# adaLN attention block: K from centred x only, 1/sigma on the scores, scale in three parts, shift by column tiles, P turned by DMA

## The chip, the core and the metric

The kernel runs on one core of a Trainium2 chip. Its engines are TensorE (PE, with its weight loads PEld), VectorE (DVE), ScalarE (ACT), GpSimd (POOL) and SyncE (SP), which issues nearly all DMAs. The engines run side by side and meet through semaphores. The metric is the device time of one execution in microseconds (us), the median of the runs.

## The reference

```python
B, N, D = (2, 256, 1152)
def reference(x, c, wqkv, wo, w_mod):
    mod = (_silu(c) @ w_mod).reshape(B, 6, 1, D)
    shift_a, scale_a, gate_a, ... = [mod[:, i] for i in range(6)]
    h = _layernorm(x, axis=-1) * (1 + scale_a) + shift_a
    qkv = h @ wqkv                                   # D x 3D
    q, k, v = (qkv[..., :D], qkv[..., D:2 * D], qkv[..., 2 * D:])
    p = _softmax(jnp.einsum('bqd,bkd->bqk', q, k) * D ** (-0.5), axis=-1)
    a = jnp.einsum('bqk,bkd->bqd', p, v) @ wo
    return x + gate_a * a
```

All tensors are bf16. The layer norm is x minus its mean, divided by sigma (with eps 1e-5). One head spans all 1152 columns. Of the six thirds of `w_mod` only shift, scale and gate of the attention are used.

## The kernel before

The 512 tokens (two batches of 256) lie in four tiles `t` of 128; batch 0 is tiles 0 and 1. The 1152 columns are nine blocks `k` of 128. PE contracts over `k`, so h is needed transposed: `hT[:, k, tokens]`.

Each engine carries out its instructions in the order in which the code states them. The wrappers `vec`, `sca`, `ten` and `spq` record every instruction of DVE, ACT, PE and SP, and `pin` (at the end) ties each list into that order. All of them therefore have the line of the wrapper, L74, in the profile; they are told apart by their tiles. POOL's instructions have their own lines. PSUM has eight banks: a pool `psum` of six and two single ones, `psum_a` and `psum_b`; a new tile waits until the tile that had its bank before has been read.

The stages, in PE's order:

- *Start.* c is loaded as 18 rows of 128, turned on PE, and made into silu(c) (`silu_c`). Twelve filler products keep PE busy meanwhile. For each tile of x, mean and variance come from DVE (`dve_stats`, `dve_aggr`) or, for tile 3, from ACT (`act_mean`, `act_var`); POOL computes 1/sigma with a power of -0.5 (L197, L198, L223 to L226); `dve_norm` writes the normalised x, PE turns it (`transposes`), and DVE or ACT copies it to `xnT`.
- *Scale.* 1 + scale is a product of w_mod's second sixth (`wS`) with silu(c), for the first four column blocks (`scale_A`) and the other five (`scale_B`), 81 products of 54 columns (silu(c) repeated 27 times).
- *K.* `scaled` writes `hTs`, the normalised x times (1 + scale), without shift: a shift adds the same amount to all scores of a query, which the softmax removes. Six of K's nine column blocks are summed in six banks at a time (`k_part`, `k_step`); two more are begun early (`early_half`, added from SBUF afterwards), and the last is a whole `k_block`.
- *Shift.* 81 products of 54 columns (`shift_block`) with `wH`, w_mod's first sixth, stand among K's last products. Then `modulated` writes `hT` from `xnT`, scale and shift, 12 of 18 half blocks on DVE and 6 on ACT.
- *Q*, nine blocks of nine products; the *scores* S, 36 products of 256 columns; *V*, twelve groups (`v_group`) of nine products of 384 columns.
- *Softmax* on DVE and ACT beside V: `row_max`, `exps`, `normalized`. P is turned by eight PE transposes ahead of the last V group, and copied to SBUF.
- *Gate.* DVE multiplies w_mod's third sixth (`wG`) with silu(c) block by block: 18 steps `gate_step` on 128 x 1152, which add into `gacc`. Twelve stand ahead of the first row maximum, two between the softmax steps, four behind. After the last one POOL sums over the partitions (two `PARTITION_ALL_REDUCE`, L558), which gives `gate_bc`, and then writes `wo_last` (L579), the last 192 columns of wo times the gate of batch 1, in nine instructions.
- *P times V*, 36 products, gives `attnT`; the *output*, per tile three chunks of 384 columns; DVE multiplies with the gate (`ga`) and adds x (`o_sb`). The last tile's last 192 columns use `wo_last`, so that they need only x; the last 64 get x by PE and are copied by ACT.

SP issues the loads in the order x, wS, wK, wH, then Q's first columns, wG, the rest of Q and V, and wo. wG takes the place of wS and wO that of wH, so these loads wait until PE has used the older weights. The stores follow on the same queue.

Of the kernel before, what the change touches and what calls it, by code (L numbers as in the profile page):

```python
# [16 lines left out]
def kernel(  # L17
# [10 lines left out]
    P = 128  # L28
# [6 lines left out]
    NCH = D // CW  # L35
    EPS = 1e-5
# [3 lines left out]
    NEARLY = 2  # L40
    WE = (NACC + NEARLY) * P
    KA = 4
    KB = KT - KA
    NR = 54
# [4 lines left out]
    wmod_v = w_mod.rearrange("(kk p) (s n) -> p kk s n", p=P, s=6)  # L49
# [6 lines left out]
    work = ctx.enter_context(tc.tile_pool(name="work", bufs=2))  # L56
    psum = ctx.enter_context(tc.tile_pool(name="psum", bufs=6, space=PSUM))
# [5 lines left out]
    pe_seq, dve_seq, act_seq, sp_seq = [], [], [], []  # L63
# [20 lines left out]
    spq = _Rec(nc.sync, sp_seq)  # L84

# [11 lines left out]

    ident = const.tile([P, P], BF16)
    nc.gpsimd.memset(ident, 0.0)
    nc.gpsimd.affine_select(  # L100
# [3 lines left out]
    junk_rhs = const.tile([P, 512], BF16)  # L104
    vec.memset(junk_rhs, 1.0)
    ones_bf = const.tile([P, P], BF16)
    nc.gpsimd.memset(ones_bf, 1.0)
    ones_row = const.tile([1, 512], BF16)
    nc.gpsimd.memset(ones_row, 1.0)
    neg_half = const.tile([P, 1], F32)  # L110
    nc.gpsimd.memset(neg_half, -0.5)

    c_sb = const.tile([2 * KT, P], BF16)
    x_sb = act.tile([P, TT, D], BF16)
    nc.scalar.preload_act_table_set("natural_log_exp_and_others")
    nc.scalar.dma_start(out=c_sb, in_=c.rearrange("b (k p) -> (b k) p", p=P))
# [4 lines left out]
    wmpool = ctx.enter_context(tc.tile_pool(name="wmpool", bufs=1))  # L123
# [8 lines left out]

    def load_k(k0, k1, c0=0, c1=D):
        spq.dma_start(out=wK[:, k0:k1, c0:c1], in_=wqkv_v[:, k0:k1, D + c0 : D + c1])

    PAIRS = ((0, 2), (2, 4), (4, 6), (6, 8), (8, 9))
    CA = KA * P
    load_x(1)
    load_x(0)
    load_x(3)  # L140
    for k0, k1 in PAIRS:
        load_mod(wS, 1, k0, k1, 0, CA)
    load_k(0, 1, 0, WE)
    load_x(2)
    for k in range(1, KA):
        load_k(k, k + 1, 0, WE)
    load_mod(wS, 1, 0, 5, CA, D)
    load_mod(wS, 1, 5, KT, CA, D)
    load_k(KA, 6)
    load_k(6, KT)  # L150
    load_k(0, KA, WE, D)
    for k0, k1 in PAIRS:
        load_mod(wH, 0, k0, k1, 0, D)


    cT_ps = psum_b.tile([P, 2 * KT], BF16, tag="pb")
    ten.transpose(cT_ps, c_sb, ident[: 2 * KT, : 2 * KT])
    junk_ps = psum_a.tile([P, 512], F32, tag="pa")

    def fillers(n):  # L160
        for _ in range(n):
            ten.matmul(junk_ps, lhsT=ident, rhs=junk_rhs, start=True, stop=True)

    fillers(12)
    e_sb = small.tile([P, 2 * KT], F32, tag="e_sb")
    sca.activation(out=e_sb, in_=cT_ps, func=ACT.Exp, scale=-1.0)
    scT_f = const.tile([P, KT, B], F32)
    scT_rep = const.tile([P, KT, NR // B, B], BF16)

    def silu_c():  # L170
        vec.tensor_scalar_add(out=e_sb, in0=e_sb, scalar1=1.0)
        vec.reciprocal(out=e_sb, in_=e_sb)
        vec.tensor_tensor(
            out=scT_f.rearrange("p k b -> p b k"),
            in0=cT_ps.rearrange("p (b k) -> p b k", b=B),
            in1=e_sb.rearrange("p (b k) -> p b k", b=B),
            op=ALU.mult,
        )
        sca.copy(out=scT_rep, in_=scT_f.unsqueeze(2).to_broadcast([P, KT, NR // B, B]))
# [3 lines left out]


    mv_all = const.tile([P, TT, 2], F32)
    rstd = const.tile([P, TT], F32)
    nb = const.tile([P, TT], F32)
    xn = act.tile([P, TT, D], BF16, tag="a1")
    xnT = act.tile([P, KT, T], BF16, tag="a2")
    stats = {t: small.tile([P, NCH, 6], F32, tag="stats", name="stats") for t in (1, 0, 2)}  # L190

    def dve_stats(t, s):
        vec.bn_stats(out=stats[t][:, s, :], in_=x_sb[:, t, s * CW : (s + 1) * CW])

    def dve_aggr(t):
        vec.bn_aggr(out=mv_all[:, t, :], in_=stats[t])
        nc.gpsimd.tensor_scalar_add(out=rstd[:, t : t + 1], in0=mv_all[:, t, 1:2], scalar1=EPS)  # L197
        nc.gpsimd.tensor_tensor(out=rstd[:, t : t + 1], in0=rstd[:, t : t + 1], in1=neg_half, op=ALU.pow)  # L198

    def dve_nb(t):  # L200
        vec.scalar_tensor_tensor(
            out=nb[:, t : t + 1], in0=mv_all[:, t, 0:1], scalar=-1.0, in1=rstd[:, t : t + 1],
            op0=ALU.mult, op1=ALU.mult,
        )

    def dve_norm(t):
        vec.tensor_scalar(
            out=xn[:, t, :], in0=x_sb[:, t, :], scalar1=rstd[:, t : t + 1], scalar2=nb[:, t : t + 1],
            op0=ALU.mult, op1=ALU.add,
        )  # L210

    ssum = small.tile([P, 1], F32, tag="ssum")
    nmean = small.tile([P, 1], F32, tag="nmean")
    ssq = small.tile([P, 1], F32, tag="ssq")

    def act_mean(t):
        sca.activation(out=xn[:, t, :], in_=x_sb[:, t, :], func=ACT.Copy, accum_out=ssum)
        sca.activation(out=nmean, in_=ssum, func=ACT.Copy, scale=-1.0 / D)

    def act_var(t):  # L220
        sca.activation(out=xn[:, t, :], in_=x_sb[:, t, :], func=ACT.Square, bias=nmean,
                       scale=1.0, accum_out=ssq)
        nc.gpsimd.tensor_scalar(out=rstd[:, t : t + 1], in0=ssq, scalar1=1.0 / D, scalar2=EPS,  # L223
                                op0=ALU.mult, op1=ALU.add)
        nc.gpsimd.tensor_tensor(out=rstd[:, t : t + 1], in0=rstd[:, t : t + 1], in1=neg_half, op=ALU.pow)
        nc.gpsimd.tensor_tensor(out=nb[:, t : t + 1], in0=nmean, in1=rstd[:, t : t + 1], op=ALU.mult)  # L226

    tps = {}
    HALF = ((0, KA), (KA, KT))

    def transposes(t, h, pool, tag):
        k0, k1 = HALF[h]
        tp = pool.tile([P, KB, P], BF16, tag=tag, name="tp")
        for k in range(k0, k1):
            ten.transpose(tp[:, k - k0, :], xn[:, t, k * P : (k + 1) * P], ident)
        tps[t, h] = tp

    def xnT_copy(t, h, on_dve):
        k0, k1 = HALF[h]
        dst, srct = xnT[:, k0:k1, t * P : (t + 1) * P], tps[t, h][:, : k1 - k0, :]  # L240
        if on_dve:
            vec.tensor_copy(out=dst, in_=srct)
        else:
            sca.copy(out=dst, in_=srct)


    s1p = const.tile([P, KT, B], F32)
    sh = const.tile([P, KT, B], F32)
# [3 lines left out]
    early = const.tile([P, NEARLY, T], F32)  # L252

    junk_mm = psum.tile([P, 512], F32, tag="mm")

    def fillers2(n):
        for _ in range(n):
            ten.matmul(junk_mm, lhsT=ident, rhs=junk_rhs, start=True, stop=True)

    psSA = psum_a.tile([P, KA - 1, NR], F32, tag="pa")  # L260
    ten.matmul(psSA.rearrange("p j r -> p (j r)"), lhsT=ones_bf[0:1, :],
               rhs=ones_row[0:1, 0 : (KA - 1) * NR], start=True, stop=False, skip_group_check=True)
    psS0 = psum_b.tile([P, NR], F32, tag="pb")
    ten.matmul(psS0, lhsT=ones_bf[0:1, :], rhs=ones_row[0:1, 0:NR], start=True, stop=False,
               skip_group_check=True)

    def scale_A(kk):
        for j in range(KA):
            ten.matmul(
                psS0 if j == 0 else psSA[:, j - 1, :], lhsT=wS[:, kk, j * P : (j + 1) * P], rhs=sc_rhs(kk),  # L270
                start=False, stop=(kk == KT - 1), skip_group_check=True,
            )

    def scale_B(kk):
        for j in range(KA, KT):
            ten.matmul(
                psSB[:, j - KA, :], lhsT=wS[:, kk, j * P : (j + 1) * P], rhs=sc_rhs(kk),
                start=(kk == 0 and j == KA), stop=(kk == KT - 1), skip_group_check=True,
            )

    def shift_block(kk):
        for j in range(KT):
            ten.matmul(
                psH[:, j, :], lhsT=wH[:, kk, j * P : (j + 1) * P], rhs=sc_rhs(kk),
                start=(kk == 0 and j == 0), stop=(kk == KT - 1), skip_group_check=True,
            )

    def one(t):
        return slice(t * P, (t + 1) * P)

    def scaled(k, sl, scalar):
        vec.tensor_scalar(out=hTs[:, k, sl], in0=xnT[:, k, sl], scalar1=scalar, scalar2=None, op0=ALU.mult)

    def k_part(k, sl, first=False):
        for f in range(NACC):
            ten.matmul(
                accs[f][:, sl], lhsT=wK[:, k, f * P : (f + 1) * P], rhs=hTs[:, k, sl],
                start=first, stop=False, skip_group_check=True,
            )
# [22 lines left out]
    def evac(idx, out_ap, in_ap):  # L322
        if idx % 2 == 0:
            return vec.tensor_copy(out=out_ap, in_=in_ap)
        return sca.copy(out=out_ap, in_=in_ap)
# [337 lines left out]
```

## Time and profile before

| | |
|---|---|
| median of 3 runs | 100.06 us (100.00 to 100.22) |
| profiled execution, first to last instruction | 99.5 us |
| PE / DVE / ACT / POOL busy | 92.7 / 66.8 / 29.3 / 24.5 us |
| DMA | 21.06 MB, in the slices up to 400 GB/s until 55 us |
| 81 Q products of 512 columns | 17.65 us from 35.16 |
| 16 gate steps `SCALAR_TENSOR_TENSOR` | 1.42 us each |
| two `PARTITION_ALL_REDUCE` | 6.89 us each |

The profiled execution is given by its span alone. A row of the timeline has the start, the time from the first to the last of the merged instructions, engine, line, operation, output <- inputs with their shapes, the number of instructions, and in brackets the engine's idle time before them and what ended it. Matmuls overlap: a 512-column product is shown with some 0.38 us, but the next one starts 0.216 us later, so spacings count and not means. In the 40 slices each digit is the busy share in tenths of 2.49 us.

### The profile page before, as it was taken

To read this page: it belongs to the slowest core of one execution; us is meant where nothing else is said; L and a number is where in the kernel's file an instruction comes from. 1 tells how busy PE (TensorE), PEld (TensorE's weight loads), DVE (VectorE), ACT (ScalarE), POOL (GpSimd) and SP (SyncE) were. 2 spreads that over 40 slices of the span, in tenths; PEclk is the share of its full clock that TensorE was granted. 3 is DMA by queue.
4 is the path that set the end of the run, shared out by engine and by line. 5 is a ranking of instruction groups with operands and counts; after the bars stand their busy time and mean duration, and the time that the engine had idled before them with its cause. 6 is when DMAs were issued, how large, how long until landed. Compare 5 with 4: busy or idle time off the path is not lost.

```text
span 99.5 us, 1843 instructions
## 1 busy us (share of the span) xinstructions
PE 92.7 (93%) x753; PEld 57.3 (58%) x753; DVE 66.8 (67%) x131; ACT 29.3 (29%) x58; POOL 24.5 (25%) x29
## 2 busy tenths in 40 slices
PE   0899999899999999999999999999999999999960
PEld 0334788894465644444447866566568766556560
DVE  1694398426063899999992999960237767879870
ACT  5340905402060494223322453323126400000000
POOL 5042043000000000000000000039999910079600
PEclk9999999999999999999999999999999999999999
DMA  2999999999999999999999300000000000302212
GB/s 59 319 259 368 403 395 407 386 394 414 382 370 389 359 403 377 342 326 327 347 410 412 127 0 0 0 0 0 0 0 10 0 0 0 119 5 114 88 70 85
DMA packets 16339, 21.06 MB, mean 212 GB/s; under 512 B 1355, under 2 KB 10827, under 8 KB 16331
## 3 DMA queue, kind: packets, MB, share of 16 engines
q1 hardware_dynamic: 16160, 20.93, 59.7%
q8 instruction: 6, 0.10, 0.4%
q10 hardware_dynamic: 171, 0.02, 0.1%
q14 instruction: 2, 0.02, 0.0%
HBM read 19.76 MB, written 1.18 MB: 210 GB/s over the span
## 4 chain that ended last, share of the span: by engine, by line
PE 86%; DVE 6%; DMA 2%; POOL 1%; issue 1%; ACT 0%; DVEq 0%
PE ps L74 59%; PE acc L74 12%; PE s_ps L74 4%; DVE stats L74 3%; PE tp L74 2%; PE psH L74 2%; DMA c_sb<-in_c_dram 2%; PE psE L74 2%; PE junk_mm L74 2%; PE psSB L74 1%; PE psSA L74 1%; DVE o_sb L74 1%; DVE ga L74 1%; POOL rstd L198 1%; DVE mv_all L74 0%
## 5 line engine op out<-in xcount | busy, mean ns | idle before, releaser
L558 POOL PARTITION_ALL_REDUCE gate_bc<-gacc x2 | 13.7, 6886 | 49.8 <-DVE gacc L74 49.8
L74 DVE SCALAR_TENSOR_TENSOR gacc<-wG,scT_f,gacc 128x1152 f32<-128x1152 bf16 x16 | 22.7, 1418 | 0.5
L74 PE MATMUL ps<-wqv,hT 128*128 128x384 bf16 x108 | 17.9, 326 | 0.0
L74 PE MATMUL ps<-hT,wqv 128*128 128x512 bf16 x81 | 17.6, 379 | 0.0
L74 PE MATMUL ps<-wO,attnT 128*128 128x384 bf16 (+1 forms) x108 | 17.0, 319 | 0.0
L74 PEld LDWEIGHTS <-attnT 128*128 128x128 bf16 x126 | 11.3, 98 | 6.4
L74 PEld LDWEIGHTS <-hT 128*128 128x128 bf16 x108 | 10.5, 98 | 6.7
L74 PEld LDWEIGHTS <-wK 128*128 128x128 bf16 x137 | 11.1, 97 | 5.8 <-issue 0.5
L74 PEld LDWEIGHTS <-wqv 128*128 128x128 bf16 x81 | 7.9, 98 | 9.6 <-DVE hT L74 0.4
L74 PE MATMUL acc<-hTs,wK 128*128 128x128 bf16 (+2 forms) x102 | 12.9, 278 | 0.4 <-DVE hTs L74 0.4
L74 ACT CAST qkT<-ps 128x512 bf16<-128x512 f32 x10 | 5.8, 583 | 10.9 <-PE ps L74 10.9
L74 DVE TENSOR_TENSOR ga<-ps,gate_bc 128x384 f32<-128x384 f32 (+1 forms) x12 | 6.5, 540 | 3.4 <-PE ps L74 3.4
L579 POOL TENSOR_TENSOR wo_last<-wO,gate_bc 128x192 bf16<-128x192 bf16 x9 | 5.9, 683 | 7.6 <-issue 7.6
L74 ACT CAST v_sb<-ps 128x384 bf16<-128x384 f32 x10 | 4.8, 478 | 9.6 <-PE ps L74 9.6
L74 DVE TENSOR_TENSOR o_sb<-ga,x_sb 128x384 bf16<-128x384 f32 (+1 forms) x12 | 7.3, 609 | 0.4
L74 PE MATMUL junk_ps<-junk_rhs,ident 128*128 128x512 bf16 x12 | 5.3, 632 | 0.0
L74 ACT CAST o_sb<-ps 128x64 bf16<-128x64 f32 x1 | 0.2, 212 | 17.3 <-PE ps L74 17.3
L74 DVE CAST v_sb<-ps 128x384 bf16<-128x384 f32 x2 | 1.1, 557 | 6.0 <-PE ps L74 6.0
L74 ACT COPY xnT<-tp 128x640 bf16<-128x640 bf16 (+1 forms) x5 | 3.1, 650 | 6.0 <-PE tp L74 6.0
L74 DVE CAST attnT<-ps 128x512 bf16<-128x512 f32 (+1 forms) x6 | 3.5, 603 | 1.8 <-PE ps L74 1.8
L74 DVE CAST qkT<-acc 128x512 bf16<-128x512 f32 x3 | 1.9, 685 | 4.1 <-PE acc L74 4.1
L74 PE MATMUL ps<-hTs,wK 128*128 128x512 bf16 x19 | 4.6, 378 | 0.0
(77 smaller groups left out, 89.7 us busy)
## 6 DMA issues: line engine op xcount, KB each, us to landing
wqv<-in_wqkv_dram SPq DMA_DIRECT2D x5, 864.0 KB, 12.1
wG<-in_w_mod_dram SPq DMA_DIRECT2D x3, 864.0 KB, 10.5
wO<-in_wo_dram SPq DMA_DIRECT2D x3, 864.0 KB, 9.2
wH<-in_w_mod_dram SPq DMA_DIRECT2D x4, 576.0 KB, 9.9
x_sb<-in_x_dram SPq DMA_DIRECT2D x4, 288.0 KB, 3.3
wS<-in_w_mod_dram SPq DMA_DIRECT2D x4, 256.0 KB, 5.9
wK<-in_wqkv_dram SPq DMA_DIRECT2D x4, 256.0 KB, 6.0
wK<-in_wqkv_dram SPq DMA_DIRECT2D x1, 864.0 KB, 10.4
```

The costliest lines, as they stand in the source:

```text
L74: r = fn(*a, **k)
L198: nc.gpsimd.tensor_tensor(out=rstd[:, t : t + 1], in0=rstd[:, t : t + 1], in1=neg_half, op=ALU.pow)
L558: ar = nc.gpsimd.partition_all_reduce(gate_bc[:, b, :], gacc[:, b, :], P, bass.bass_isa.ReduceOp.add)
L579: nc.gpsimd.tensor_tensor(out=wo_last[:, k, :], in0=wO[:, k, D - TAILW :], in1=gate_bc[:, B - 1, D - TAILW :], op=ALU.mult)
```

## The change

- *c* is loaded with its 1152 values spread over the partitions as p*9 + k (256 pieces of 18 bytes), so that no PE transposition is needed; w_mod's rows are read in the same order.
- *x is only centred.* `centre` subtracts the mean; tile 0's mean comes from DVE, tiles 1 and 2's from ACT, tile 3's from DVE. Variances come later: two from the same statistics, two from `act_var` beside K. K is the product of centred x times (1 + scale): it lacks the factor 1/sigma of its token.
- *1/sigma on the scores.* POOL computes 1/sigma of all tokens, splits it into three bf16 parts, PE turns these (12 x 128), DVE masks them, and one PE product spreads the sum of the three over all partitions: `rstd_bc`. `scores` multiplies S by it, column by column (the key's token), before the maximum. For Q and V, `normalised` multiplies `hTs` by it into `hT`.
- *Scale in three parts* of two, three and four column blocks (PA, PB, PC), with 32 instead of 54 columns. K starts after the first part.
- *Shift by column tiles.* silu(c) (32 columns) is the stationary operand and `wH` the moving one: per row block four products of 288 columns, each into 32 of the 128 partitions of `psH`. DVE transposes the result in 32 x 32 blocks to `shT`.
- *The first three Q blocks* are computed from `hT` before the shift is there; the shift times their weights (27 products of 2 columns) is added as a bias when they are copied. Then `shifted` adds the shift to `hT` in place, for the other Q blocks and for V.
- *P is turned by DMA*: four transposing transfers on SP's queue.
- *Orders.* The first Q columns are loaded before wH; K's last block is finished behind the shift; nine gate steps stand ahead of the scores' maxima, one between the probabilities, eight behind; all V groups follow each other. POOL's instructions are pinned too. P times V, the output and `wo_last` are as before.

```diff
-    wmod_v = w_mod.rearrange("(kk p) (s n) -> p kk s n", p=P, s=6)
+    wmod_v = w_mod.rearrange("(p kk) (s n) -> p kk s n", kk=KT, s=6)
...
-    nc.scalar.dma_start(out=c_sb, in_=c.rearrange("b (k p) -> (b k) p", p=P))
+    sca.dma_start(out=c_sb, in_=c.rearrange("b (p k) -> p b k", k=KT))
...
+    load_x(0)
     load_x(1)
-    load_x(0)
+    load_x(2)
+    load_s(PA, 0, 4)
+    load_s(PA, 4, KT)
+    load_k(0, 1)
     load_x(3)
...
+    load_k(1, 2)
+    load_s(PB, 0, 4)
...
+    load_chunk(0, 0, 5)
+    load_chunk(0, 5, KT)
+    for k0, k1 in ((0, 3), (3, 6), (6, KT)):
         load_mod(wH, 0, k0, k1, 0, D)
...
+    def centre(t, scalar, op):
+        vec.tensor_scalar(out=xc[:, t, :], in0=x_sb[:, t, :], scalar1=scalar, scalar2=None, op0=op)
...
+    fillers(11)
     silu_c()
...
+    mv0 = bn(0)
+    centre(0, mv0[:, 0:1], ALU.subtract)
+    act_mean(1)
+    centre(1, nmean[:, 1:2], ALU.add)
+    act_mean(2)
+    scale_open(PA, psum_a, "pa")
+    transposes(0, 0, psum, "mm")
+    transposes(0, 1, psum, "mm")
+    fillers(2)
+    scale_rows(PA, 0, 4)
...
+    fillers(2)
+    scale_rows(PA, 4, KT)
+    xcT_copy(1, 1, False)
+    scaled(0, tok(0), psS[PA][:, 0, 0:1])
...
+    act_var(1)
+    act_var(2)
+
+    for k in range(PB[0], PB[1] - 1):
+        k_step(k)
+
+
+    scale_open(PC, psum_b, "pb")
+    scale_rows(PC, 0, KT)
...
+    gps.tensor_scalar_add(out=rstd, in0=var, scalar1=EPS)
+    gps.tensor_tensor(out=rstd, in0=rstd, in1=neg_half, op=ALU.pow)
...
+    k_step(PC[0] - 1)
+    k_step(PC[0])
+    pT3 = psum_a.tile([NP3, P], BF16, tag="pa", name="pT3")
+    ten.transpose(pT3, parts.rearrange("p t i -> p (t i)"), ident)
+    masked = const.tile([NP3, TT, P], BF16)
+    vec.tensor_tensor(out=masked, in0=pT3.unsqueeze(1).to_broadcast([NP3, TT, P]), in1=mask, op=ALU.mult)
+    k_step(PC[0] + 1)
+    bc_ps = psum_a.tile([P, T], F32, tag="pa", name="bc_ps")
+    ten.matmul(bc_ps, lhsT=junk[:NP3, :P], rhs=masked.rearrange("p t n -> p (t n)"), start=True, stop=True)
+    sca.copy(out=rstd_bc, in_=bc_ps)
+
+    def normalised(k):
+        vec.tensor_tensor(out=hT[:, k, :], in0=hTs[:, k, :], in1=rstd_bc, op=ALU.mult)
+
+    for k in range(KT):
+        normalised(k)
+    for k in range(PC[0] + 2, KT):
         k_step(k)
...
+    q_first = [q_block(f, hT) for f in range(FB)]
...
+    for kk in range(KT):
+        for j in range(4):
+            ten.matmul(psH[32 * j : 32 * j + 32], lhsT=sc_rhs(kk), rhs=wH_v[:, kk, :, j, :],
+                       start=(kk == 0), stop=(kk == KT - 1))
+    shT = const.tile([P, KT, 32], F32)
+    vec.transpose(out=shT.rearrange("p k c -> p (k c)"), in_=psH.rearrange("p k c -> p (k c)"))
...
+    k_block(LASTF, ps, KA, KT)
+    last_k = ps
...
+            vec.tensor_scalar(out=hT[:, k, tok(b)], in0=hT[:, k, tok(b)], scalar1=shT[:, k, b : b + 1],
+                              scalar2=None, op0=ALU.add)
...
+    for f in range(FB):
+        for b in range(B):
+            if b == 0:
+                sca.activation(out=qkT[:, f, tok(b)], in_=q_first[f][:, tok(b)], func=ACT.Identity,
+                               bias=qb[:, f, b : b + 1], scale=1.0)
...
+    gates = [(b, kt) for g in range(0, KT, 3) for b in range(B) for kt in range(g, g + 3)]
...
+        p_fs[b] = work.tile([P, NQ, N], F32, tag="p_f", name="p_f")
+        vec.tensor_tensor(out=p_fs[b], in0=s_tiles[b],
+                          in1=rstd_bc[:, tok(b)].unsqueeze(1).to_broadcast([P, NQ, N]), op=ALU.mult)
         mx = small.tile([P, NQ], F32, tag="mx")
...
+    def turn(b):
+        pT = work.tile([P, NQ, N], BF16, tag="pT")
+        for i in range(NQ):
+            spq.dma_start_transpose(out=pT[:, :, i * P : (i + 1) * P], in_=pns[b][:, i, :])
+        pT_sbs.append(pT)
...
-    N_G = B * KT
-    for i in range(N_G - 6):
-        gate_step(i)
-    row_max(0)
+    gate_steps(9)
+    scores(0)
     exps(0)
-    gate_step(N_G - 6)
-    row_max(1)
+    scores(1)
     exps(1)
-    normalized(0)
-    gate_step(N_G - 5)
-    normalized(1)
-    for i in range(N_G - 4, N_G):
-        gate_step(i)
+    probs(0)
+    turn(0)
+    gate_steps(1)
+    probs(1)
+    turn(1)
+    gate_steps(len(gates))
     gate_done = dve_seq[-1].ins.name
```

## The prediction

> **What bounds the kernel now.** I read the page first, part 1 and the slices, then the chain of work that ended last, then the timeline of DVE, POOL and PE.
>
> Part 1 and the slices (busy tenths, 40 slices of 2.49 us each):
>
> ```profile
> PE 92.7 (93%) x753; PEld 57.3 (58%) x753; DVE 66.8 (67%) x131; ACT 29.3 (29%) x58; POOL 24.5 (25%) x29
> ...
> PE   0899999899999999999999999999999999999960
> ...
> DVE  1694398426063899999992999960237767879870
> ACT  5340905402060494223322453323126400000000
> POOL 5042043000000000000000000039999910079600
> ```
>
> TensorE has no gap after its start. The chain of waits, in order of time (start, us, what), says where that start is set and how it ends:
>
> ```profile
> 8.26 0.03 issue
> 8.29 0.31 PE psSA L74
> ...
> 12.27 0.30 DVE hTs L74
> 12.57 0.04 issue
> 12.62 0.82 PE acc L74 x6
> ...
> 52.80 3.93 PE s_ps L74 x36
> 56.73 16.09 PE ps L74 x99
> 72.82 0.45 PE pT_ps L74 x8
> 73.27 21.49 PE ps L74 x144
> 94.76 0.02 issue
> ```
>
> K's first product is at 12.62, and from there one matmul follows another to the tail. The timeline (start, us) shows what is nearly as late as TensorE, and does not appear in that chain:
>
> ```profile
> 36.71 0.81 DVE L74 TENSOR_SCALAR gacc<-wG,scT_f 128x1152 f32<-128x1152 bf16 x1
> 37.56 11.60 DVE L74 SCALAR_TENSOR_TENSOR gacc<-wG,scT_f,gacc 128x1152 f32<-128x1152 bf16 x8
> 60.51 5.78 DVE L74 SCALAR_TENSOR_TENSOR gacc<-wG,scT_f,gacc 128x1152 f32<-128x1152 bf16 x4
> 66.42 13.69 POOL L558 PARTITION_ALL_REDUCE gate_bc<-gacc  x2 [49.75 <-DVE gacc L74]
> 87.71 5.87 POOL L579 TENSOR_TENSOR wo_last<-wO,gate_bc 128x192 bf16<-128x192 bf16 x9 [7.59 <-issue]
> 95.33 0.67 PE L74 MATMUL ps<-wo_last,attnT 128*128 128x128 bf16 x9
> ```
>
> The last gate step ends at 66.3. POOL then reduces for 13.7 us, stands still for 7.6 us without a releaser, and multiplies nine slices of wo_last until 93.6. TensorE wants the first slice at 95.1 and the ninth half a microsecond later. So POOL's chain, 27.2 us behind the last gate step, has about 2 us to spare. That is the second bound.
>
> **The change, part by part.** The profiled execution has a span of 99.5; the median, 100.06, lies 0.54 above, and I add this at the end. T below is the moment when the last shift product is in PSUM.
>
> *Start of K.* The transposition of c on PE and the wait for it go (c lands at 2.75, exp starts at 3.03). c now comes in 256 pieces of 18 bytes: between 2.75 as before and 4.1 if it lands with the x loads beside it (0.76 + 3.3); I take 3.3. The four small steps take 1.0 as before: scT_f at 4.3. Only one tile's statistics stand ahead now (1.40 + 0.24), then centring (0.58, row xn): 6.5. The second tile's mean on ACT (0.6 + 1.16 + 0.2 + 0.2) ends there too; centring 7.1. The transposes (0.50 a tile), half of the scale rows and the copies (0.42) interleave; the third centring ends near 9.3, the first scaling (0.29) at 9.6. The first row of wK is the sixth load, issued near 3.2, and took 6.0 to land before: 9.2. K starts at 10.0. The ends are 9.6, and 11.4 if matmuls still run at the rate of the first fillers (5.30 us for 12, 0.43 each, against 0.216 later).
>
> *K to the first Q blocks.* 74 of K's 81 block products lie here (the last block's seven follow later): 74 x 0.216 = 16.0. Transposes 18 x 0.055 = 1.0. Scale products of parts two and three: 63 x 0.0256 (45 in 1.15), with openings, 1.7. The two products that spread 1/sigma over the partitions: 0.3. Sum 19.0. New waits on PE's queue, everything behind each held up: wK's second row, tile 3's centring, two PSUM copies before transposes, and `parts` from POOL. The last comes after two variances on ACT (1.45 each) and nine small POOL steps (0.27 apart, the power 0.72). I count 1.2 in all, between 0.3 and 2.5.
>
> *Nine multiplications by 1/sigma on DVE.* Nearest row: 128x512 with two inputs, 0.69; 6.2 in all, done about 7.1 after the spread product. PE has 5.65 of other work and then eats one k per 0.216, so k=8 is wanted at 7.4. Covered with 0.3 to spare; each 0.1 us more per instruction would cost PE 0.6.
>
> *Three Q blocks without shift*: 27 x 0.216 = 5.8, only moved.
>
> *Shift by column tiles.* 81 products of 2.06 (0.92 + 0.23 + 0.91) go; 36 of 288 columns come, four to disjoint 32-column strips. One of 288 takes 0.122 (256 take 0.109). No row shows two products at once: 4.4 one after another, 1.1 four abreast. I take 1.5, near the low end, as each of four has its own columns, weights and output partitions, and none waits for another; 4.4 is a rival. The Trainium skill, TensorE: Matmul & The Clock Gate, "Part 3: Packing small matmuls — row/col tiling", gives three column tiles 2.38 times the speed; by that ratio alone the stage would take 4.4 / 2.38 = 1.8, an estimate, and the end would move 0.3.
>
> So T = 10.0 + 19.0 + 1.2 + 5.8 + 1.5 + 0.2 (drain) = 37.7.
>
> *DVE behind T.* This is the part that decides. The 32x32 transposition of 288 columns: between 0.18 (18 columns) and 0.69 (512), taken 0.45. Copy 0.17. Twelve additions in place 2.65 (ten took 2.65 with two scalars; one scalar ran at 0.205 each). Bias copy 0.17, last K addition 0.7, three half evacuations of Q 1.4 to 1.7, each behind ACT's half. Together 5.8: gates start at 43.5, where they started at 36.7. Nine gate steps, 2 x 0.84 + 7 x 1.45 = 11.8: 55.3. The first scores are there at T + 1.5 (last K block) + 0.7 (27 bias products) + 0.1 + 11.7 (54 Q products) + 2.1 = 53.8, so DVE, not PE, is late. `scores` now has one multiplication of 0.69 more: 2 x (0.69 + 0.69 + 0.17) = 3.1: 58.4. Twelve gate steps stood ahead of the first maximum before, nine stand there now, so eight instead of four are left for the end. Then probabilities 0.8, one gate 1.45, probabilities 0.8, eight gates 11.6: the last ends at **73.0**, 6.7 later than before. Behind them on DVE wait two V copies (v_sb blocks 8 and 10), whose PSUM buffers the sixth tile after each, about 74, needs again: no stall.
>
> *POOL behind the gates.* 0.1 + 13.7 + 7.6 = 21.4: wo_last starts at 94.4. The 7.6 has no releaser in the profile; wO landed long before (issued 44 to 48, 9.2 to land) and the reduction had ended. It lies between two kinds of POOL instruction, and both kinds stay in this order. The Trainium skill, GPSIMD Engine Reference, "2.1 Instruction dispatch", says that the first call of a freshly loaded kernel pays about 6 us with no visible instruction. The gap in this trace, 7.59, is longer; by the page's figure the end would come 1.6 earlier, an estimate. Nine slices take 5.87 beside DVE's work; the undisturbed ones 0.51 apart, 4.6. DVE is nearly done by then: 4.8. Last slice at 99.2.
>
> *Tail.* From the last slice: semaphore and one product 0.1, ten products of 64 columns 0.3, drain 0.2, copy 0.25, and from the copy's end to the span's end 3.0 (96.53 to 99.5). PE has then stood still for 5 us and may run at the fillers' rate, 0.25. In all 4.1: span 103.3.
>
> *P by DMA.* Eight PE transposes (0.45) and two copies go. Four transfers come on SP's queue, behind wO and ahead of the stores. They wait for P at about 59 and 62, and are wanted at 73 and 75. Nothing waits behind them until the first store. One of 64 KB takes between 2.1 (the 288 KB store) and 12.1 (the slowest landing of the page, 864 KB of wqv); I take the store, the transfer nearest in size that also starts from SBUF. Four in series are then done at 70: hidden. A gain is excluded, as PE is not last.
>
> *Loads.* The same bytes; SP's order puts the first Q columns ahead of wH and a third of wG ahead of the second. The first 10.0 MB, up to wH, are moved by 29 (the slices' GB/s added up) and landed by 30.5; wH is wanted at 36. Hidden, with 5 us to spare; if that is gone, T moves by the lack. Nothing of wG, wqv or wO is wanted before 39.
>
> *The sum.* TensorE alone: scores end at T + 17.9, V 17.6 (99 products in 16.09 and nine more), P times V 3.9, output up to wo_last 16.7 (78.4 to 95.1): T + 56.1 = 93.8, 1.3 earlier than now, and an end at 98.3. But POOL lets it go at 99.2, so the span is 103.3, 3.8 above the old one: 99.5 + 3.8 + 0.54 = **103.8**.
>
> **The rivals.**
> - *Faster: POOL's still time goes.* If the 7.6 were something that need not recur, wo_last would start at 86.8 and TensorE would be last: 98.3 + 0.54 = 98.8. It decides from about 5 us off POOL's chain. For it: no releaser is shown. Against: it stands between the two kinds of instruction, which remain. 9%.
> - *Column tiles run one after another.* T is 40.6, everything behind DVE shifts: 106.7. For it: no pair of products overlaps in this trace. 18%.
> - *DMA turns P slowly.* At 12.1 each, in series, P is there at 59 + 48 = 107 and the end 23 later, 130; it decides from 4 each. For it: no row shows such a transfer. Against: the stores' 2.1. 4%.
> - *No change* (POOL about 3.5 short of my sum): 2%.
>
> **How the numbers follow.** My case has 67%. Its low end is 101.2, all open terms low (K 0.4, waits 0.9, tiles 0.4, DVE 0.4, slices 0.2, tail 0.25); all high would add 4.4 (K 1.4, waits 1.3, DVE 0.6, slices 1.1), of which I take 1.7, as they are independent: 105.5. With the serial tiles the range is 101.2 to 107.3; it leaves out the faster case, the slow transfers and the tie. This kernel's runs differ by 0.2%, so that much can be told from none. Faster 9%, same 2%, slower 89%.
>
> **What would show it.** K's first product near 10; the shift within 1.1 to 2; gates from 43 to 73 on DVE with no idle before the scores; the reduction from about 73; a still POOL for 7.6; wo_last from about 94; PE idle for 4 to 5 us just before the last products; P's transfers landed before 70. The prediction is wrong if gates end before 69, or if POOL has no pause.

## The result and the profile after

The changed kernel takes 103.16 us (median of 4 runs, 103.06 to 103.39); the kernel before takes 100.14 in the same comparison (100.00 to 100.50). The ratio is 1.0294, with a 95 % interval from 1.0266 to 1.0321: slower, by 3.0 us, where 103.8 was predicted. The profiled execution has a span of 101.5 and a time of its own of 103.2. Here and below medians are over all executions, while ratios leave out those more than 1.5 % above the fastest of their kernel.

The first part of the page and the slices (tenths of 2.54 us each):

```profile
PE 92.8 (92%) x697; PEld 54.6 (54%) x697; DVE 75.6 (74%) x139; ACT 30.5 (30%) x63; POOL 25.5 (25%) x33
...
PE   4958999999999999999999999999999999999450
...
DVE  1396873071899409999999999999585999999710
...
POOL 6400000280000000000000000000799996006950
PEclk9999999999999999999999999999999999999965
```

TensorE begins earlier than before, and now has a gap at the end (digits 4 and 5 in slices 38 and 39), where POOL is busy (6, 9, 5). VectorE is busy for 8.8 us more (75.6 against 66.8); 3.8 of them come from the rows of `o_sb` (11.1 us against 7.3), the first of which is held up (see the last section). The end of the chain of waits names what decides (start, us, what):

```profile
69.99 1.43 DVE gacc L76
71.46 0.18 issue
71.69 6.72 issue
78.41 6.92 POOL gate_bc L76
85.40 7.52 POOLq L667
92.92 4.86 POOL wo_last L76 x8
97.82 0.81 PE ps L76 x11
98.66 0.21 ACT o_sb L76
```

Before, this stretch was TensorE alone. Now it is the last gate step on DVE, the two all-reduces (the first of them under "issue"), POOL's still time, the products of wo_last, and only then TensorE. The same places in the timelines of PE, DVE and POOL:

```profile
9.89 0.81 PE L76 MATMUL acc<-hTs,wK 128*128 128x256 bf16 x6 [0.38 <-DVE hTs L76]
...
36.55 1.29 PE L76 MATMUL psH<-wH,scT_rep 128*32 128x288 bf16 x36
...
60.06 11.34 DVE L76 SCALAR_TENSOR_TENSOR gacc<-wG,scT_f,gacc 128x1152 f32<-128x1152 bf16 x8
...
71.64 13.69 POOL L76 PARTITION_ALL_REDUCE gate_bc<-gacc  x2 [48.55 <-DVE gacc L76]
92.21 5.56 POOL L76 TENSOR_TENSOR wo_last<-wO,gate_bc 128x192 bf16<-128x192 bf16 x9 [6.88 <-issue]
...
93.87 0.28 PE L76 MATMUL ps<-wo_last,attnT 128*128 128x128 bf16 x2
...
97.82 0.27 PE L76 MATMUL ps<-wo_last,attnT 128*128 128x128 bf16 x1 [0.24 <-POOL wo_last L76]
```

TensorE was ready for wo_last at 93.87 and got the ninth slice at 97.8; in between it took the slices one by one, as POOL wrote them. The last gate step ends 5.1 us later than before (71.4 against 66.3). POOL's still time was 0.7 shorter and its products 0.3, so that the last slice is 4.2 later. POOL had been about 2 us ahead of TensorE there before, and TensorE's last product now ends 2.3 later (98.6 against 96.3).

### The profile page after: what moved, and what is told of

Its sections match the earlier page's. It is cut to its first block, busy times and chain, and to the rows that moved or that the text cites. A ratio compares the mean times of both kernels' runs of the same rounds, so it can differ in the third digit from the quotient of the medians.

```text
span 101.5 us, 1751 instructions
## 1 busy us (share of the span) xinstructions
PE 92.8 (92%) x697; PEld 54.6 (54%) x697; DVE 75.6 (74%) x139; ACT 30.5 (30%) x63; POOL 25.5 (25%) x33
## 3 DMA queue, kind: packets, MB, share of 16 engines
HBM read 19.76 MB, written 1.18 MB: 206 GB/s over the span
## 4 chain that ended last, share of the span: by engine, by line
DVE 36%; PE 23%; POOL 14%; issue 8%; POOLq 7%; ACT 5%; DMA 3%
DVE gacc L76 23%; POOLq L667 7%; POOL gate_bc L76 7%; PE acc L76 6%; PE psQ L76 6%; POOL wo_last L76 5%; PE psK L76 3%; DMA c_sb<-in_c_dram 3%; ACT xc L76 2%; PE tp L76 2%; DVE hT L76 2%; DVE qkT L76 2%; DVE mx L76 1%; DVE stats L76 1%; POOL rstd L76 1%
## 5 line engine op out<-in xcount | busy, mean ns | idle before, releaser
L76 PE MATMUL psQ<-hT,wqv 128*128 128x512 bf16 x81 | 17.8, 379 | 0.0
L76 PE MATMUL ps<-wqv,hT 128*128 128x384 bf16 x108 | 17.7, 326 | 0.0
L76 PEld LDWEIGHTS <-wK 128*128 128x128 bf16 x109 | 9.2, 98 | 8.0 <-issue 0.9
L76 PE MATMUL acc<-hTs,wK 128*128 128x512 bf16 (+2 forms) x78 | 13.0, 314 | 0.4 <-DVE hTs L76 0.4
L76 DVE TENSOR_TENSOR o_sb<-ga,x_sb 128x384 bf16<-128x384 f32 (+1 forms) x12 | 11.1, 928 | 0.4
L76 DVE TENSOR_TENSOR hT<-hTs,held 128x512 bf16<-128x512 bf16 x9 | 5.5, 685 | 1.9 <-ACT held L76 1.9
L76 PE MATMUL junk_ps<-junk 128*128 128x512 bf16 x15 | 5.5, 520 | 1.5 <-DVE junk L76 1.5
L76 ACT CAST qkT<-psQ 128x512 bf16<-128x512 f32 x6 | 3.5, 586 | 6.8 <-PE psQ L76 6.8
L76 ACT ACTIVATE hT<-hT,shT 128x256 bf16<-128x256 bf16 x6 | 2.5, 496 | 10.1 <-DVE shT L76 10.1
L76 PEld LDWEIGHTS <-junk 128*128 128x128 bf16 (+2 forms) x19 | 2.1, 120 | 5.2 <-issue 3.6
L76 PE MATMUL psK<-hTs,wK 128*128 128x512 bf16 x21 | 4.9, 380 | 0.0
## 6 DMA issues: line engine op xcount, KB each, us to landing
wqv<-in_wqkv_dram SPq DMA_DIRECT2D x5, 864.0 KB, 11.4
wG<-in_w_mod_dram SPq DMA_DIRECT2D x3, 864.0 KB, 11.4
```

The source lines that it names most:

```text
L76: r = fn(*a, **k)
```

## The experiments

All are edits of the changed kernel. The theory is the prediction's: gates, all-reduces, pause and wo_last set the end, and TensorE alone would be done about 3 us sooner than was measured. Spans are those of the profiled execution. The changed kernel's four executions have spans of 101.3 to 101.7. `pool_switch`, `skip2` and `one_strip` were executed once each; what they move, 2.3 to 12.1 us, is far more than that.

**wo_last taken away.** The last tile's last 192 columns then get gate and x from VectorE, like the others.

```diff
-    for k in range(KT):
-        gps.tensor_tensor(out=wo_last[:, k, :], ...)
...
-            last = (t == TT - 1) and (ci == len(chunks) - 1)
-            pregated = (t == TT - 1) and c0 >= D - TAILW
+            last = pregated = False
```

> The changed kernel without wo_last: the last tile's last 192 columns use wo like the others, and the gate and x come from VectorE at the end. Theory A (GpSimd's chain behind the last gate step sets the end): TensorE no longer stops before the last products, so it ends near 95 instead of 98.6, with a tail of gate and x on VectorE of some 0.7 us more; the span falls from 101.5 to about 98.5 to 99.5 and the time from 103.2 to about 99.5 to 100.5. Theory B (TensorE or the new transfers are slower all along and the stop is only a symptom): the time stays within 1 us of 103.2.

106.49 us (105.91 to 109.44), 1.0551 times the kernel before (1.0459 to 1.0642): neither theory. The timelines of POOL and PE at the start say why:

```profile
9.78 0.28 POOL L76 TENSOR_SCALAR_AFFINE_SELECT ident<-ident 128x128 bf16<-128x128 bf16 x1 [8.79 <-issue]
...
15.40 0.94 PE L76 MATMUL acc<-hTs,wK 128*128 128x256 bf16 x6 [0.39 <-DVE hTs L76]
```

POOL stood still for 8.79 us ahead of its first instruction that is not a memset, which comes at 1.28 in the changed kernel. TensorE waited 4.6 us for what POOL writes next (`ones_row`), its transposes and fillers then ran at a slower rate (two fillers in 1.06 instead of 0.59), and K began 5.5 us late. With wo_last gone, the all-reduces are POOL's last work, and the next execution starts with the other kind. By this reading the edit moved the pause from the end to the start. The next run tests it and repeats the experiment.

**The same, with one small POOL product left behind the all-reduces.**

```diff
-    for k in range(KT):
-        gps.tensor_tensor(out=wo_last[:, k, :], ...)
+    gps.tensor_tensor(out=rest, in0=rstd, in1=rstd, op=ALU.mult)
```

> The nine wo_last products go, the last tile is gated on VectorE like the others, and one small POOL product (128x4) stays behind the all-reduces, so that POOL ends the program on its ordinary instructions. If late code on POOL at the start was what moved everything by 5.5 us in the run without it, K starts near 9.9 again (it was 15.4). Theory of the prediction (TensorE alone would be 1.3 us faster than before, POOL's chain takes that and 3.2 more): no TensorE idle before the last tile, its last product near 95, VectorE's last step near 96.3, span 98.7 (98.2 to 99.3), which is 2.8 below the changed kernel and within 0.5 of the kernel before. Rival (the time is lost before the gates, in TensorE's own work): the span stays above 100.5.

Span 98.8, time 100.55, ratio to before 1.001 (0.9976 to 1.0044). From the timelines of PE, POOL and DVE:

```profile
10.00 0.81 PE L76 MATMUL acc<-hTs,wK 128*128 128x256 bf16 x6 [0.38 <-DVE hTs L76]
...
77.08 17.76 PE L76 MATMUL ps<-wO,attnT 128*128 128x384 bf16 x126
...
92.43 0.19 POOL L76 TENSOR_TENSOR rest<-rstd 128x4 f32<-128x4 f32 x1 [7.07 <-issue]
...
96.01 0.23 DVE L76 TENSOR_TENSOR o_sb<-ga,x_sb 128x64 bf16<-128x64 f32 x1
```

K starts at 10.0 again, so the late start belonged to POOL's last kind of instruction. TensorE runs without a stop to 94.8, then DVE is last. With no product of wo_last to wait for, the changed kernel has the time of the kernel before: the 2.7 us between 98.8 and 101.5 lie in POOL's chain, and not in TensorE's work.

**An ordinary POOL product between the two all-reduces.**

```diff
+        if b == 1:
+            gps.tensor_tensor(out=rest, in0=rstd, in1=rstd, op=ALU.mult)
         ar = gps.partition_all_reduce(gate_bc[:, b, :], ...)
```

> The changed kernel with one small elementwise product (128 x 4) put on GpSimd between the two all-reduces. If the pause of 6.9 us ahead of wo_last is paid for going from one kind of GpSimd instruction to the other, it is paid here once more ahead of the small product, and something like it on the way back to the second reduction: the second reduction starts 12 to 16 us later than 78.4 and the end moves by as much, to 114 to 119 us. If the pause belongs to the end of the second reduction or to a port that VectorE holds, the second reduction starts less than 1 us later and the end stays within 1 us.

115.69 us, span 113.6. The timeline of POOL:

```profile
71.58 6.85 POOL L76 PARTITION_ALL_REDUCE gate_bc<-gacc  x1 [48.54 <-DVE gacc L76]
85.21 0.49 POOL L76 TENSOR_TENSOR rest<-rstd 128x4 f32<-128x4 f32 x1 [6.78 <-issue]
91.47 6.85 POOL L76 PARTITION_ALL_REDUCE gate_bc<-gacc  x1 [5.76 <-issue]
105.31 4.60 POOL L76 TENSOR_TENSOR wo_last<-wO,gate_bc 128x192 bf16<-128x192 bf16 x9 [6.99 <-issue]
```

A product of 0.5 us costs 13.1 on POOL (wo_last starts at 105.31 instead of 92.21) and 12.1 at the end (its slices take 1.0 less): each change of kind pays again, 6.78 one way and 5.76 the other. That settles the rival by which the still time need not recur.

**Two of the 18 gate steps left out** (this leaves out two of the nine blocks in the sum of batch 1's gate).

```diff
-    gate_steps(len(gates))
+    gate_steps(len(gates) - 2)
```

> The changed kernel with the last two of 18 gate steps left out (the gate then lacks two of nine row blocks for batch 1). Theory A: the last gate step ends 2.86 us earlier, near 68.6, and the whole chain and the end follow one for one: span 98.6 to 98.9, just before TensorE would be last. If TensorE bounds the end: unchanged at 101.5.

100.92 us, span 99.2. POOL's timeline:

```profile
68.71 13.69 POOL L76 PARTITION_ALL_REDUCE gate_bc<-gacc  x2 [45.63 <-DVE gacc L76]
89.97 5.71 POOL L76 TENSOR_TENSOR wo_last<-wO,gate_bc 128x192 bf16<-128x192 bf16 x9 [7.58 <-issue]
```

The all-reduces start 2.9 earlier, wo_last 2.2 (the pause was 0.7 longer this time), and the span is 2.3 shorter. Work on DVE ahead of the all-reduces is paid nearly one for one.

**Shift in one column strip.** Of the 36 products, the four of the first row block keep their strips, and the other 32 all go to the first strip. This leaves out most of the sums of the other three strips, so the shift is wrong.

```diff
+            r = j if kk == 0 else 0
-            ten.matmul(psH[32 * j : 32 * j + 32], ...)
+            ten.matmul(psH[32 * r : 32 * r + 32], ...)
```

> The changed kernel with the shift's 36 products of 288 columns, but 32 of them into the first of the four column strips (the shift is then wrong). If the four strips work side by side in the changed kernel, these 32 run one after another at 0.122 us and the shift takes about 4.1 us instead of 1.25; VectorE's gates and with them the end move by about 2.8 us, span near 104.3. If the strips do not overlap and a product is simply short, the shift stays at 1.3 us and the end where it is.

106.11 us, span 104.4. The timelines of PE and POOL:

```profile
36.49 4.22 PE L76 MATMUL psH<-wH,scT_rep 128*32 128x288 bf16 x36
...
74.49 13.69 POOL L76 PARTITION_ALL_REDUCE gate_bc<-gacc  x2 [51.47 <-DVE gacc L76]
95.32 5.39 POOL L76 TENSOR_TENSOR wo_last<-wO,gate_bc 128x192 bf16<-128x192 bf16 x9 [7.13 <-issue]
```

36 products of the same size take 4.22 when 32 of them share a strip and 1.29 in four strips: the strips work side by side. The 2.9 us reach the all-reduces as 2.85 and the span as 2.9: T passes to the end whole, through DVE and POOL. The Trainium skill, TensorE: Matmul & The Clock Gate, "Part 3: Packing small matmuls — row/col tiling", has 2.38 times for three column tiles; four gave about 4.22 / 1.29 = 3.3 here. No run has three.

**P turned on TensorE again**, ahead of V's last group; the DMA part of the change is undone.

```diff
-            spq.dma_start_transpose(out=pT[:, :, i * P : (i + 1) * P], in_=pns[b][:, i, :])
+            for j in range(NQ):
+                ten.transpose(pT_ps[:, j, i * P : (i + 1) * P], pns[b][:, i, j * P : (j + 1) * P], ident)
```

> P is turned on TensorE again (8 transposes, two copies, one on ScalarE and one on VectorE, ahead of V's last block) instead of by four transfers. Theory (the transfers are hidden and TensorE is not last): the same time as the changed kernel, 102.9 to 103.5, span 101.2 to 101.8; TensorE has 0.45 us more to do and as much less idle time before wo_last. Rival (the transfers lengthen the path, or the transposes would): a difference of 0.5 us or more.

103.05 us (102.72 to 103.53), ratio 1.025 (1.0185 to 1.0316), span 101.1: as the changed kernel. wo_last starts at 92.44 there, and TensorE is ready for it at 94.42 instead of 93.87, still ahead of the ninth slice. The part neither gains nor costs here; TensorE's 0.45 come out of its idle time.

**All gate steps ahead of the softmax.**

```diff
-    gate_steps(9)
+    gate_steps(len(gates))
     scores(0)
```

> All 18 gate steps stand ahead of the softmax, nothing else changes. Theory: the last gate step ends near 67.2 (71.4 in the changed kernel), the all-reduces run 67.4 to 81.1, wo_last starts near 88.1 and TensorE no longer waits for it. The price is on P: the scores' steps come at 67.3, P is written near 72.3 and landed at 75.5 to 76.5, where TensorE wants it at about 73, so TensorE stops for some 2 us there: span 98.0 if that is hidden, 100.2 if not; up to 103 if the all-reduce also holds VectorE's softmax steps off, as it does the first o_sb. Rival (the order of the gates does not set the end): wo_last late by the same wait, span 101.5.

113.14 us (111.45 to 113.20), ratio 1.1164 (1.103 to 1.1298), span 111.5: the expectation missed the price by far (at most 103 had been expected), and the gain too. The timelines of DVE and POOL, and PE's row for V among the groups of instructions (after the bar: busy, mean ns; then idle before it and what ended it):

```profile
69.92 4.61 DVE L76 TENSOR_SCALAR nmx<-mx 128x2 f32<-128x2 f32 x1
...
69.39 13.92 POOL L76 PARTITION_ALL_REDUCE gate_bc<-gacc  x2 [46.30 <-DVE p_f L76]
90.25 5.25 POOL L76 TENSOR_TENSOR wo_last<-wO,gate_bc 128x192 bf16<-128x192 bf16 x9 [6.94 <-issue]
...
L76 PE MATMUL ps<-wqv,hT 128*128 128x384 bf16 x108 | 22.5, 378 | 8.6 <-DVE p_f L76 6.1 <-ACT v_sb L76 2.5
```

The last gate step ends at 67.04, as expected, but the all-reduces start only at 69.39, and the profile puts this wait down to the scores' step (`p_f`); why they wait for it stays open. So POOL is 2 us earlier and not 4, and TensorE no longer waits for it. The price is on V. TensorE stops for 6.1 us because V's next groups need PSUM banks that the scores hold until DVE has read them, which the expectation did not see. It stops for 2.5 us more for ACT's copies of V, which stand behind exponentials that wait for a step on 128 x 2 numbers on DVE: that step takes 4.61 beside the first all-reduce (0.17 elsewhere). And V's products after the first stop run at a granted clock of 0.5 to 0.8 and take 22.5 us in all instead of 17.7. Moving the whole softmax behind the gates does not pay.

**Two gate steps in DVE's idle time before the shift.** DVE waits from 34.2 to 37.9 for the shift, and wG's first third is there. In the first version seven steps stay ahead of the scores, `gacc` has a buffer of its own, and wo_last holds only 64 columns, the next 128 being gated on DVE:

```diff
+    gacc = act.tile([P, B, D], F32, tag="gacc")
...
+    gate_steps(2)
+
     psH = psum_b.tile([P, KT, 32], F32, tag="pb", name="psH")
...
-    gate_steps(9)
+    gate_steps(7)
...
-    TAILW = CW // 2
+    TAILW = LASTW
```

> Two of the 18 gate steps go into VectorE's idle time before the shift (34.2 to 37.9 in the changed kernel), and wo_last holds only the last 64 columns (nine products of 128x64 on POOL), the 128 columns before them being gated on VectorE. Theory: gates end near 69.2, all-reduces 69.3 to 83.0, pause near 7, wo_last from 90.1 to about 92.6, before TensorE wants it (about 94.5): TensorE ends near 95.0, VectorE near 95.9, span 98.0 to 98.8, time 99.7 to 100.5, within 0.4 % of the kernel before. Rival (POOL's pause is as long as what is left over): TensorE still waits for wo_last, span above 100.

100.95 us (100.31 to 102.40), ratio 1.0017 (0.9979 to 1.0056), span 100.3. Of its ten executions this is one of four with spans of 100.3 to 100.7; the other six have 98.6 to 99.2, where 98.0 to 98.8 was expected. The timelines of DVE, POOL and PE:

```profile
55.45 0.69 DVE L76 TENSOR_TENSOR p_f<-s_ps,held 128x512 f32<-128x512 f32 x1 [1.77 <-PE s_ps L76]
...
73.28 13.69 POOL L76 PARTITION_ALL_REDUCE gate_bc<-gacc  x2 [48.54 <-DVE gacc L76]
93.95 3.12 POOL L76 TENSOR_TENSOR wo_last<-wO,gate_bc 128x64 bf16<-128x64 bf16 x9 [6.97 <-issue]
...
11.61 0.81 PE L76 MATMUL acc<-hTs,wK 128*128 128x256 bf16 x6 [0.38 <-DVE hTs L76]
```

Two things spoil the expectation. This execution started K 1.6 us late, with two fillers taking 1.06 at 8.1 (0.59 at 7.6 where K starts at 10.0); no other execution of this version has a trace. And DVE now waits 1.77 + 0.35 for the scores: with seven steps ahead of them, 2.2 us less, DVE, which had been late by about half a microsecond, came early, and the two saved steps turned into a wait. So the two steps have to come off the end of the list. Nine ahead again, first without wo_last (as above, with the small product), then with its 64 columns:

```diff
-    gate_steps(7)
+    gate_steps(9)
```

> Two gate steps go into VectorE's idle time before the shift and nine stay ahead of the scores, so seven instead of eight or nine come at the end; wo_last is replaced by the small POOL product. Theory: the scores come 0.6 later on VectorE (54.9), which TensorE does not feel; the last gate step ends near 69.2, so the second all-reduce lets the first o_sb go near 81.7 instead of 84.0, VectorE catches up with TensorE before the end, and the last o_sb follows TensorE's last product (94.8) by 0.7: span 98.1 (97.8 to 98.6), which is 0.7 below the version without the two early steps (98.8) and 0.5 below the kernel before. Rival (with POOL's chain gone, TensorE alone sets the end and the early steps change nothing): 98.8.

> As gates9_no_wo, but wo_last stays, for the last 64 columns only. Theory: last gate step near 69.2, all-reduces to 83.1, pause 7, nine products of 128x64 from 90.1 to 93.2, ahead of TensorE, which wants the first near 94.5; the 320 columns before them are gated on VectorE until 96.0: span 98.3 to 98.9. TensorE has no wait for wo_last. Rival (the pause grows when POOL comes earlier): TensorE waits, span above 99.5.

Without wo_last: 100.34 us, ratio 0.9966 (0.9939 to 0.9993), span 98.6, 0.2 below the version without the two early steps, where 0.7 was forecast: DVE did catch up with TensorE, but the six steps of the last three chunks, 1.66 in a row, still end 1.3 after TensorE's last product. With 64 columns of wo_last: **100.02 us** (99.82 to 100.11) against 100.64 for the kernel before in that comparison (99.82 to 101.35), ratio 0.9944 (0.9913 to 0.9975), span 98.3. Its timelines of DVE, POOL and PE:

```profile
34.21 0.81 DVE L76 TENSOR_SCALAR gacc<-wG,scT_f 128x1152 f32<-128x1152 bf16 x1
35.05 1.42 DVE L76 SCALAR_TENSOR_TENSOR gacc<-wG,scT_f,gacc 128x1152 f32<-128x1152 bf16 x1
...
69.37 13.69 POOL L76 PARTITION_ALL_REDUCE gate_bc<-gacc  x2 [46.23 <-DVE gacc L76]
89.95 2.79 POOL L76 TENSOR_TENSOR wo_last<-wO,gate_bc 128x64 bf16<-128x64 bf16 x9 [6.89 <-issue]
...
94.43 0.43 PE L76 MATMUL ps<-wo_last,attnT 128*128 128x64 bf16 x9
```

The all-reduces start 2.3 earlier, POOL is done at 92.7, TensorE takes its last products without a wait, and TensorE is last again. This is the fastest version that was run, and it keeps every part of the change; by the ratio it is 0.6 % below the kernel before, whose single executions reach down to 99.82 too.

## Why the prediction was right, and where it was off

The sign, the place and the size came out (the range of 101.2 to 107.3 holds 103.16), and the mechanism is the predicted one: the change makes TensorE's work shorter and DVE's longer, and what DVE does before its last gate step goes through POOL to the end. Step by step:

| step | predicted | measured |
|---|---|---|
| c landed / K's first product | 3.3 / 10.0 | 3.8 / 9.89 |
| nine multiplications by 1/sigma | 6.2 | 5.51 |
| shift products | 1.5 | 1.29 |
| T | 37.7 | 37.9 |
| T to the first gate step | 5.8 | 4.9 |
| last gate step ends | 73.0 | 71.4 |
| all-reduces and still time | 21.4 | 20.8 |
| TensorE ready for wo_last | 93.8 | 93.87 |
| nine slices, last one done | 4.8, 99.2 | 5.56, 97.8 |
| from there to the end | 4.1 | 3.7 |
| span | 103.3 | 101.5 |

- **T.** Right to 0.2, since small errors offset each other: from K's first product to the shift's first it took 26.7 where 26.0 was summed, and the shift with its drain 1.3 instead of 1.7. c landed 0.5 later than taken, but within its range, and K still began at 9.89. The upper end for K's start, 11.4 with slow matmuls, did occur once: in the execution of `early2_wo64` nine transposes took 1.14 instead of 0.68, and K began at 11.61. The column tiles work abreast.
- **DVE behind T.** The 5.8 up to the first gate step was 0.9 too long. The prediction placed each of Q's half evacuations on DVE behind ACT's half; the three waited for nothing, and from the first of them to the first gate step it took 1.18 (1.4 to 1.7 had been taken). The twelve additions took 2.34 instead of 2.65. Small steps that overlap make up the rest. The gate steps came 1.42 apart, not 1.45. Together the last gate step was 1.6 early. That DVE and not TensorE would be late for the first scores was right (no idle time in front of them), but by so little that two steps fewer turned it round.
- **POOL.** The pause was taken at 7.59 from the one row there was; in these runs the pauses between an all-reduce and an ordinary product are 6.78 to 7.59. The slices took 5.56, not 4.8: DVE was not "nearly done" beside them, since its first o_sb had been held up (below). In `pool_switch`, where DVE was through by 104.4 and the slices began at 105.31, they took 4.60.
- **Tail.** The nine products of 64 columns took 0.67 instead of 0.43, at a granted clock of 0.5 to 0.6 in the last two slices; the prediction had put 0.25 on that. TensorE's wait was not one gap of 4 to 5 us but seven short ones, 2.3 in all, between 93.87 and 97.8.
- **P by DMA.** Hidden, as forecast: four transfers of 2.4 to 4.4 us from issue to landing, all there before 68. The 12.1 of the slow-transfer rival was far from it.
- **The baseline.** The sum ended 1.8 too long, and the time only 0.6, because a second term was wrong the other way: that the time came out so close is in part luck. The profiled execution of before (99.5) was set 0.54 below the median of other executions. In each single execution the time is 1.7 to 1.9 above the span (2.1 in one), and the later executions of before have spans from 98.0 to 99.5, with a median of 98.8: the page showed one of the longest. Rightly the sum would have stood against about 98.4 with 1.7 on top, and "1.3 earlier" of TensorE's work is then 0.1 to 0.5, which is what the last version shows (98.3, ratio 0.9944). The 2 us to spare, and the differences of 5.1, 4.2 and 2.3 us above, are likewise against this one long execution. Why the spans of before vary by 1.5 us stays open: only one of them has a trace.
- **The range.** Its upper end takes 1.7 of the 4.4 us of high terms "as they are independent", without a working (the root of the sum of their squares is 2.3), while its lower end takes all low terms in full. The result lies well inside.
- **Rivals.** Faster by a vanishing pause: refuted by the product between the all-reduces. Strips one after another: refuted by 4.22 against 1.29. Slow turning of P: refuted by landings of 2.4 to 4.4. TensorE's own end of 98.3 was met to the digit once POOL was early, but with another last tile (64 columns of wo_last instead of 192), so the digit is luck.

## What to carry to other kernels

Before moving work to an engine that is "67 % busy", follow what its last instruction releases: here 27 us of reductions, pause and products on POOL hang behind the last gate step, with 2 us to spare, and the chain of waits of the kernel before does not show it. A saving on the engine that is last is worth no more than the slack of the second chain, and a cost on the second chain counts nearly in full once the slack is gone. When work is taken out of such a chain for an experiment, look at the start of the execution too: what an engine ends with can be paid when the program runs again.

## What the runs showed that was not expected

- **POOL's change of kind seems to be paid across executions.** It took 6.8 to 7.6 us from all-reduces to ordinary products, 5.76 back, and 8.79 at the start where POOL's last work in the program was an all-reduce. One product of 0.19 us behind the all-reduces took the pause away from the start (K at 10.0 instead of 15.4). The Trainium skill, GPSIMD Engine Reference, "2.1 Instruction dispatch", gives about 6 us with no visible instruction for the first call of freshly loaded code. The traces agree in kind; of the sizes only the 5.76 is as short. That code is loaded in these pauses is the page's explanation; the traces show the pause and when it comes.
- **The all-reduce holds DVE up.** The first o_sb in the changed kernel, and in the one with two gate steps left out:

```profile
79.36 4.65 DVE L76 TENSOR_TENSOR o_sb<-ga,x_sb 128x384 bf16<-128x384 f32 x1
...
79.35 1.73 DVE L76 TENSOR_TENSOR o_sb<-ga,x_sb 128x384 bf16<-128x384 f32 x1
```

  It took 4.65 us instead of 0.56 (79.36 to 84.01) beside the second all-reduce, recorded until 85.33. With the all-reduces 2.9 earlier it took 1.73 (until 81.08, all-reduce until 82.40), with 2.3 earlier 2.33: the release is each time some 1.3 us before the recorded end. In the kernel before, where the second all-reduce ended at 80.11 and the first o_sb began at 80.82, it took 0.56. Copies out of PSUM ran at their usual 0.55 to 0.69 beside the first one. The Trainium skill, GPSIMD Engine Reference, "8. Key points", speaks of contention with DVE instructions that have two SBUF inputs or are in a mode with two ports. o_sb is of the first sort. The steps held up with the gates first (4.61 on 128 x 2 numbers, and 5.01 in the scaling of P) have one such input beside a scalar; whether they use two ports no trace shows. In the changed kernel the delay is hidden behind POOL's pause; in the version with the small product DVE runs without a stop from the held o_sb to the end, 1.4 after TensorE, and so is last because of it.
